# A fused attention and two-layer gated kernel: another computed order for the first half, and two first gates in banks of their own

## The chip, the cores and the metric

One NeuronCore of a Trainium2 chip runs the whole program. Its engines are TensorE (PE), VectorE (DVE), ScalarE (ACT), GpSimd (POOL) and SyncE (SP, which issues nearly all DMAs). Each takes its instructions in the order in which the program lists them and waits on semaphores. The metric is the device time of one execution in microseconds.

## The reference

```python
scores = scale * q @ k.T                     # (4 batch, 8 heads, 576, 576), head_dim 64
mask   = last 32 positions (heads 0-3) or last 32 of every 4th position (heads 4-7)
attn   = exp(scores - max); attn /= sum + 1e-9
x      = (attn @ v), heads side by side      # (2304 tokens, 512)
a = x @ w1;  b = x @ w2;  h = (a * b) @ w3   # 512 -> 1024 -> 1024
x = h @ w_out                                # 1024 -> 512
g = x @ w_gate                               # 512 -> 1536
out = (silu(g) * (x @ w_val)) @ w_out2       # 1536 -> 512
```

All is float32, and the kernel keeps more precision than one pass in float32r gives: each operand is split into a high and a low part, and each product is three matmuls (high x high, high x low, low x high), in the function `mm3`.

## The kernel before

Two heads make a pair; 4 batch rows of 4 pairs are the 16 units of attention. Only a band is computed: 9 blocks of 64 queries against 96 keys. A unit is: scores on PE (36 small matmuls into 2 banks), masks and maxima on DVE, exps on ACT, sums, inverse and normalisation on DVE or POOL, three groups of transposes on PE, copies of these on ACT (`pt`), values on PE (36 to 40 matmuls into 2 banks), and the evacuation into `x` in two parts (ACT the high, DVE the low; a copy to `beyond` for columns that belong to the next chunk). In the first batch row the last four of the nine softmax columns go by way of POOL and one wide exp (`WIDE`), and all normalisation is on DVE (`NORMV`); after it, normalisation is on POOL.

The tokens are taken in five chunks (4 of 512 columns and one of 256). For each chunk and each of 8 blocks k of 128 hidden units a gate is made: 12 matmuls of w1 and 12 of w2, 512 columns each (`gate`: ACT copies a to `ta`, DVE multiplies, ACT and DVE split the result to `p`), and `contraction` adds 12 matmuls with W = w3 @ w_out. W itself is made first on PE in two halves (`w_steps`, parts 0 and 1: 96 matmuls each, from 8 steps j times 4 banks), into the banks `acc` (bk_81 to bk_84), and copied out by ACT and DVE to W. The gates' banks are `ba` and `bb` (bk_85, bk_86); attention uses these and `batt` (bk_87, bk_88) until the first gate takes two away (`retire`).

Weights come as blocks of 1 MB (two weights each) in a packed form. `conversion` turns a block: a shift and a combining on DVE and a rescaling on ACT restore float32, then ACT makes the high and DVE the low part. The first two blocks go in halves of 512 columns. Buffers are `raw` (2) and `early` (2). Later blocks belong to the second layer: `quarter_block` restores them, forms sums (DVE), splits them into two `stages` (ACT and POOL) and stores them to DRAM, in `QUARTERS` portions by chunk.

The order of all this, up to the end of the third chunk, is not that of the source. `node` records each piece with an engine, a duration, what it comes after and a due time (`key`). `run_nodes` plays these through a list of events: each engine takes the ready piece with the least due time, and the pieces are then issued in the order in which they were started:

```python
                        for i in sorted(ready[e], key=lambda i: (wanted[i], i)):
...
                            started.append(i)
                            free[e] = t + x["us"]
```

The rest (`stage1` for the last two chunks, and the second layer, whose products go by a Strassen-like scheme of 7) is written out in the source's order. The second layer fills PE from about 420 us to the end and is not touched.

Of the kernel before, what the change touches and what calls it, by code (L numbers as in the profile page):

```python
# [50 lines left out]
W_BLOCKS = [("wo1", 0, 10), ("w3a", 0, 4), ("w1", 0, 0), ("w1", 1, 1), ("wo1", 2, 11), ("w3a", 2, 5), ("w1", 2, 2),  # L51
            ("wo1", 4, 6), ("w3a", 4, 8), ("w1", 3, 3), ("wo1", 6, 7), ("w3a", 6, 9),
# [36 lines left out]
QUARTERS = [2, 5, 5, 4, 2]  # L89
DMA_RATE = 0.31  # L90
FIRST, EACH, START = 4, 5, 36.0
W_AT = [24, 27]
# [4 lines left out]
def moe_chain_kernel(tc, q_in, k_in, v_in, w_in, mask_in, out):  # L97
# [8 lines left out]
    with static as st, other as ot, psum as pp, dram as dp:  # L106
# [142 lines left out]
        with att2_pool as a2:  # L249
# [239 lines left out]
            def node(engine, us, f, *args, after=(), key=INF, mb=0.0, take=None, give=None, retire=False):  # L489

                nodes.append(dict(
                    engine=engine, us=us, f=f, args=args, after=[a for a in after if a is not None], key=key, mb=mb,
                    take=take, give=give, retire=retire, got=None,
                ))
                return len(nodes) - 1
# [8 lines left out]

            def run_nodes(stock):
# [8 lines left out]
                ready = {}  # L514
                free = {}
# [7 lines left out]

                for i, x in enumerate(nodes):
                    ready.setdefault(x["engine"], [])
                    free[x["engine"]] = 0.0
                    if not left[i]:
                        push(0.0, "ready", i)
                done, started = 0, []
                while events:  # L530
                    t = events[0][0]
                    while events and events[0][0] <= t + 1e-9:
# [3 lines left out]
                        elif kind == "end":  # L536
                            done += 1
                            for g in nodes[i]["give"] or ():
                                src, items = g
# [8 lines left out]
                    for e in ready:  # L548
                        if free[e] > t + 1e-9:
                            continue  # L550
                        for i in sorted(ready[e], key=lambda i: (wanted[i], i)):
                            x = nodes[i]
                            if x["retire"] and any(b not in stock["bank"] for b in (2, 3)):
                                continue
                            if x["take"] and len(stock[x["take"][0]]) < x["take"][1]:
                                continue
                            if x["retire"]:
                                for b in (2, 3):
                                    stock["bank"].remove(b)
# [4 lines left out]
                            free[e] = t + x["us"]  # L564
                            push(free[e], "free", i)
                            if x["mb"]:
                                dma_free = max(t + 1.5, dma_free) + x["mb"] / DMA_RATE
                                push(dma_free + 1.0, "end", i)
                            else:
                                push(free[e] + 0.12, "end", i)  # L570
                            break
                assert done == len(nodes), [(nodes[i]["f"].__name__, nodes[i]["args"]) for i in range(len(nodes)) if i not in started][:9]
# [44 lines left out]
            raw_use = [None] * 4  # L617
# [3 lines left out]
            def conversion(n, key=INF, after=()):  # L621
# [4 lines left out]
                for b in range(2) if n < 2 else (None,):  # L626
                    bs = slice(0, 2) if b is None else slice(b, b + 1)
                    cols = 1024 if b is None else 512
                    ld = node("SP", 0.47, load_weights, n, b, after=[raw_use[r], *after], mb=cols / 1024, key=key)
# [9 lines left out]
                raw_use[r] = ends[-1]  # L639
# [35 lines left out]
            pt_use = [None]  # L675
            x_at, x_use = {c: [] for c in range(NC)}, {c: [] for c in range(NC)}
# [8 lines left out]
            def attention(i, t, dt, after=(), mask=None):  # L685

                b, hp = divmod(i, NPAIR)
                s_mm = node("PE", 1.05, scores, i, after=[loads["q", i], *s_use.get(sc_of(i), []), *after], key=t, take=("bank", 2))
# [653 lines left out]
```

## Time and profile before

| | |
|---|---|
| median of 3 runs | 835.08 us (833.55 to 836.95) |
| profiled execution | 835.79 us |
| span from the first to the last instruction in it | 834.0 us |
| mean granted clock of PE | 0.989 |
| PE busy | 807.8 us (97%) |
| DVE, ACT, POOL busy | 545.0, 423.6, 101.5 us |
| HBM read, written | 160.81 MB, 42.47 MB |

The span is cut into 40 slices of 20.85 us on the page. A line of waits says which instruction (engine, output, line) waited for which. In a timeline each row is a run of like instructions on one engine, and the bracket is the idle time ahead of it and what ended it. A product of 512 columns is listed with 0.39 us, since matmuls overlap; what counts is the distance from one start to the next.

### The profile page before, as it was taken

How to read it: one execution, taken by the hardware profiler on the slowest of the kernel's cores; microseconds unless marked ns; L12 is line 12 of the kernel's file. 1: busy time of each engine (PE TensorE's matmuls, PEld its weight loads, DVE VectorE, ACT ScalarE, POOL GpSimd, SP SyncE). 2: the span in 40 equal slices, each digit the busy share in tenths (PEclk: the TensorE clock that was granted, in tenths of full speed). 3: DMA queues.
4: the chain of work that ended last, by engine and by line, in shares of the span. 5: the costliest groups of instructions: out<-in, count | busy, mean ns of one | idle time of the engine just before them, and what ended most of it. 6: DMA issues, size and time to landing. Idle time of an engine off the chain costs nothing.

```text
span 834.0 us, 13900 instructions
## 1 busy us (share of the span) xinstructions
PE 807.8 (97%) x5242; PEld 732.4 (88%) x5242; DVE 545.0 (65%) x980; ACT 423.6 (51%) x975; POOL 101.5 (12%) x132
## 2 busy tenths in 40 slices
PE   6799999999999999999999999999999999999997
PEld 3677788878778788888999999999999999999997
DVE  5899967475668433475765737497746577564867
ACT  3877656666567544343554635363544354353432
POOL 1001102755554600000000000000000000000000
PEclk8799999999999999999999999999999999999999
DMA  8987454979789731277699777788978787977725
GB/s 237 313 324 257 142 185 140 301 274 319 233 311 329 246 100 73 80 247 234 233 310 386 250 253 264 244 323 277 307 251 253 246 259 244 316 270 246 252 83 176
DMA packets 80530, 204.18 MB, mean 245 GB/s; under 512 B 5840, under 2 KB 41808, under 8 KB 75856
## 3 DMA queue, kind: packets, MB, share of 16 engines
q1 hardware_dynamic: 78736, 200.68, 71.8%
q10 hardware_dynamic: 1728, 2.62, 0.9%
q8 instruction: 41, 0.67, 0.3%
q14 instruction: 25, 0.20, 0.1%
HBM read 160.81 MB, written 42.47 MB: 244 GB/s over the span
## 4 chain that ended last, share of the span: by engine, by line
PE 75%; DVE 11%; DMA 7%; ACT 3%; issue 2%; POOL 1%; SPq 0%; ACTq 0%; POOLq 0%; DVEq 0%
PE bk L195 24%; PE bk L197 23%; PE bk L196 23%; DMA raw<-w_in 6%; PE bk L382 2%; DVE raw L187 2%; PE bk L364 1%; DVE w L178 1%; PE bk L295 1%; DVE s L306 1%; DMA x2d<-o 1%; POOL stage L878 1%; DVE sm L318 1%; DVE early L187 1%; ACT s L323 1%
## 5 line engine op out<-in xcount | busy, mean ns | idle before, releaser
L195 PE MATMUL bk<-x,w 128*128 128x512 f32 (+2 forms) x400 | 147.1, 368 | 1.2 <-ACT ta L214 0.7
L197 PE MATMUL bk<-x,w 128*128 128x512 f32 (+2 forms) x400 | 144.8, 362 | 0.9 <-DVE w L178 0.9
L196 PE MATMUL bk<-x,w 128*128 128x512 f32 (+2 forms) x400 | 144.5, 361 | 0.0
L195 PEld LDWEIGHTS bk<-x,w 128*128 128x128 f32 x400 | 75.3, 188 | 12.3 <-ACT ta L214 0.9
L197 PEld LDWEIGHTS bk<-x,w 128*128 128x128 f32 x400 | 75.3, 188 | 11.7 <-DVE w L178 1.4
L1209 DVE TENSOR_TENSOR acc<-bk,acc 128x384 f32<-128x384 f32 x102 | 56.0, 555 | 44.3 <-PE bk L197 44.0
L196 PEld LDWEIGHTS bk<-x,w 128*128 128x128 f32 x400 | 75.4, 188 | 9.5
L197 PE MATMUL bk<-po,wo 128*128 128x384 f32 x240 | 80.5, 335 | 0.0
L196 PE MATMUL bk<-po,wo 128*128 128x384 f32 x240 | 80.2, 335 | 0.0
L195 PE MATMUL bk<-po,wo 128*128 128x384 f32 x240 | 79.4, 336 | 0.3 <-DVE acc L1209 0.3
L878 POOL TENSOR_TENSOR stage<-raw,stage 128x256 fp32r<-128x256 f32 x96 | 70.5, 767 | 37.4 <-ACT stage L876 37.4
L195 PE MATMUL bk<-w 128*128 128x384 f32 (+1 forms) x216 | 73.1, 341 | 0.0
L196 PE MATMUL bk<-w 128*128 128x384 f32 (+1 forms) x216 | 73.1, 338 | 0.0
L197 PE MATMUL bk<-w 128*128 128x384 f32 (+1 forms) x216 | 72.5, 339 | 0.0
L1134 ACT ACTIVATE u<-bk 128x384 f32<-128x384 f32 x80 | 38.6, 488 | 52.3 <-PE bk L197 52.3
L162 ACT ACTIVATE po<-u 128x768 fp32r<-128x768 f32 (+1 forms) x64 | 50.9, 803 | 26.3 <-PE bk L197 10.5
L163 DVE TENSOR_TENSOR po<-u,po 128x768 fp32r<-128x768 f32 (+1 forms) x64 | 57.5, 903 | 8.7 <-ACT po L162 8.6
L197 PE MATMUL bk<-p,W 128*128 128x512 f32 (+1 forms) x160 | 58.3, 369 | 0.0
L196 PE MATMUL bk<-p,W 128*128 128x512 f32 (+1 forms) x160 | 58.3, 369 | 0.0
L323 ACT ACTIVATE s<-s,sm 128x96 f32<-128x96 f32 x124 | 44.7, 363 | 26.3 <-DVE sm L318 26.3
L195 PE MATMUL bk<-p,W 128*128 128x512 f32 (+1 forms) x160 | 58.0, 379 | 0.0
L1148 ACT ACTIVATE g<-g 128x384 f32<-128x384 f32 x54 | 28.1, 521 | 40.2 <-DVE g L1143 40.1
(148 smaller groups left out, 1738.3 us busy)
## 6 DMA issues: line engine op xcount, KB each, us to landing
w<-wd SPq DMA_DIRECT2D x70, 512.0 KB, 4.6
wo<-wod SPq DMA_DIRECT2D x63, 512.0 KB, 4.6
raw<-w_in SPq DMA_DIRECT2D x28, 1024.0 KB, 7.4
mid<-wd SPq DMA_DIRECT2D x42, 512.0 KB, 4.6
wd<-stage SPq DMA_DIRECT2D x16, 896.0 KB, 4.9
early<-w_in SPq DMA_DIRECT2D x8, 1024.0 KB, 6.7
wod<-stage SPq DMA_DIRECT2D x8, 896.0 KB, 6.0
wd<-u SPq DMA_DIRECT2D x8, 896.0 KB, 5.1
```

The costliest lines, as they stand in the source:

```text
L162: nc.scalar.activation(hi, src, AF.Copy)
L163: return nc.vector.tensor_tensor(out=lo, in0=src, in1=hi.bitcast(F32), op=ALU.subtract)
L187: nc.vector.scalar_tensor_tensor(out=lo, in0=hi, scalar=3, in1=lo, op0=ALU.logical_shift_left, op1=ALU.bitwise_or)
L195: nc.tensor.matmul(ps, wh, xh, start=start, stop=False, skip_group_check=onto)
L196: nc.tensor.matmul(ps, wh, xl, start=False, stop=False, skip_group_check=onto)
L197: nc.tensor.matmul(ps, wl, xh, start=False, stop=stop, skip_group_check=onto)
L323: nc.scalar.activation(s[:, n], s[:, n], AF.Exp, bias=m[:, 0, n:n + 1], accum_out=m[:, 1, n:n + 1])
L382: nc.tensor.matmul(banks_of[got[w]][j * D:(j + 1) * D, lo - w * half:hi - w * half], v_of(i)[:KW, n, j * D:(j + 1) * D], pt[:KW, c, z * QB ...
L878: nc.gpsimd.tensor_tensor(out=dst[:, :, 1], in0=src, in1=dst[:, :, 0].bitcast(F32), op=ALU.subtract)
L1134: nc.scalar.activation(t, src, AF.Copy)
L1148: nc.scalar.activation(dst, src, AF.Silu)
L1209: nc.vector.tensor_tensor(out=a, in0=ps, in1=a, op=ALU.add)
```

## The change

The planner plays events by other rules, and some pieces are cut otherwise:

- Durations of scores, transposes and values are longer; PE's pieces take double time after a stretch with gaps; DMAs have two rates, and 8 of them at most are under way; each engine has its own latency to the next; DVE and POOL pieces marked `shared` are not started while the other engine holds such a piece.
- Due times get 40 sets of random shifts, each drawn from a seed in a list (`NUDGES`).
- The weights of w1 and w2 for k = 0, 1, 2 are loaded first, and three gates come before the first steps of W. The first two gates use bk_81 to bk_84 instead of bk_85 and bk_86, and each of their matmul groups is four pieces (3 matmuls) that need only one pair of heads each.
- `QUARTERS` goes from 2, 5, 5, 4, 2 to 3, 5, 5, 4, 1. The first gate of the fourth chunk and the last contraction of the third come into the planner, and the fourth chunk is drained through four buffers.

On DVE, in the softmax of the first pairs (s_107 is pair 0, s_116 pair 2; bk_87 and bk_88 hold pair 2's scores), the list before has:

```order
L351 RECIPROCAL sm_112<-sm_112 128x5
L306 SCALAR_TENSOR_TENSOR s_116<-bk_87,mask 128x384
L306 SCALAR_TENSOR_TENSOR s_116<-bk_87,mask 64x96
L306 SCALAR_TENSOR_TENSOR s_116<-bk_88,mask 128x384
L306 SCALAR_TENSOR_TENSOR s_116<-bk_88,mask 64x96
L356 TENSOR_TENSOR s_107<-s_107,sm_112 128x480
```

and now:

```order
L354 RECIPROCAL sm_112<-sm_112 128x5
L359 TENSOR_TENSOR s_107<-s_107,sm_112 128x480
L309 SCALAR_TENSOR_TENSOR s_116<-bk_87,mask 128x384
L309 SCALAR_TENSOR_TENSOR s_116<-bk_87,mask 64x96
L309 SCALAR_TENSOR_TENSOR s_116<-bk_88,mask 128x384
L309 SCALAR_TENSOR_TENSOR s_116<-bk_88,mask 64x96
```

Pair 0's last normalisation has moved ahead of pair 2's four mask steps.

Further on DVE, up to the last normalisation of the fourth pair (s_117; raw_77 and raw_78 are halves of loaded weights), before:

```order
L350 TENSOR_SCALAR sm_115<-sm_115 128x4
L351 RECIPROCAL sm_115<-sm_115 128x4
L185 TENSOR_SCALAR raw_77<-raw_77 128x512
L178 TENSOR_TENSOR W_74<-raw_77,W_74 128x512
L178 TENSOR_TENSOR w<-raw_78,w 128x512
L185 TENSOR_SCALAR raw_78<-raw_78 128x512
L350 TENSOR_SCALAR sm_115<-sm_115 128x5
L351 RECIPROCAL sm_115<-sm_115 128x5
L356 TENSOR_TENSOR s_117<-s_117,sm_115 128x384
L187 SCALAR_TENSOR_TENSOR raw_77<-raw_77 128x512
L187 SCALAR_TENSOR_TENSOR raw_78<-raw_78 128x512
L356 TENSOR_TENSOR s_117<-s_117,sm_115 128x480
```

and now:

```order
L353 TENSOR_SCALAR sm_115<-sm_115 128x4
L354 RECIPROCAL sm_115<-sm_115 128x4
L181 TENSOR_TENSOR w<-raw_77,w 128x512
L348 TENSOR_REDUCE sm_115<-s_117 128x5
L359 TENSOR_TENSOR s_117<-s_117,sm_115 128x384
L353 TENSOR_SCALAR sm_115<-sm_115 128x5
L354 RECIPROCAL sm_115<-sm_115 128x5
L188 TENSOR_SCALAR raw_77<-raw_77 128x512
L359 TENSOR_TENSOR s_117<-s_117,sm_115 128x480
```

Four of the six weight steps that stood between these softmax steps have gone behind them; a sum (TENSOR_REDUCE) now stands among them.

On PE, from the last transposes of pair 2 (s_116) through its values (v_104) to the first of the fourth pair (s_117), before:

```order
L364 MATMUL bk_88<-ident,s_116 96x128 x3
L382 MATMUL bk_85<-pt,v_104 64x64 x8
L382 MATMUL bk_86<-pt,v_104 64x32 x2
L382 MATMUL bk_85<-pt,v_104 64x32 x2
L382 MATMUL bk_86<-pt,v_104 64x64 x8
L195 MATMUL bk_81<-W_74,w 128x512
L196 MATMUL bk_81<-W_74,w 128x512
L197 MATMUL bk_81<-W_74,w 128x512
L195 MATMUL bk_82<-W_74,w 128x512
L196 MATMUL bk_82<-W_74,w 128x512
L197 MATMUL bk_82<-W_74,w 128x512
L364 MATMUL bk_87<-ident,s_117 96x128 x3
```

and now:

```order
L367 MATMUL bk_86<-ident,s_116 96x128 x3
L198 MATMUL bk_81<-x_76,w 128x512
L199 MATMUL bk_81<-x_76,w 128x512
L200 MATMUL bk_81<-x_76,w 128x512
L385 MATMUL bk_86<-pt,v_104 64x64 x8
L385 MATMUL bk_87<-pt,v_104 64x32 x2
L385 MATMUL bk_86<-pt,v_104 64x32 x2
L385 MATMUL bk_87<-pt,v_104 64x64 x8
L367 MATMUL bk_88<-ident,s_117 96x128 x3
L198 MATMUL bk_81<-x_76,w 128x512
L199 MATMUL bk_81<-x_76,w 128x512
L200 MATMUL bk_81<-x_76,w 128x512
```

Two groups of W's product (W_74 times w) are replaced by the first two pieces of the first gate (x_76 times w), one of which stands ahead of the values. The fourth pair's values come three groups of products after the list's start now, and four before.

The core of the diff:

```diff
-W_BLOCKS = [("wo1", 0, 10), ("w3a", 0, 4), ("w1", 0, 0), ("w1", 1, 1), ("wo1", 2, 11), ("w3a", 2, 5), ("w1", 2, 2),
-            ("wo1", 4, 6), ("w3a", 4, 8), ("w1", 3, 3), ("wo1", 6, 7), ("w3a", 6, 9),
+W_BLOCKS = [("w1", 0, 0), ("w1", 1, 1), ("w1", 2, 2), ("wo1", 0, 10), ("w3a", 0, 4), ("w1", 3, 3), ("wo1", 2, 11), ("w3a", 2, 5),
+            ("wo1", 4, 6), ("w3a", 4, 8), ("wo1", 6, 7), ("w3a", 6, 9),
...
-QUARTERS = [2, 5, 5, 4, 2]
-DMA_RATE = 0.31
+QUARTERS = [3, 5, 5, 4, 1]
+DMA_RATE = 0.285, 0.33
+LATENCY = {"PE": 0.16, "ACT": 0.1, "DVE": 0.09, "POOL": 0.05, "SP": 0.0}
...
-W_AT = [24, 27]
+EARLY = 18, 22
...
+            def nudge(seed):
+
+                r = np.random.default_rng(seed)
+                share, us = 10 ** r.uniform(-3, -0.7), 10 ** r.uniform(-0.3, 1.2)
+                kinds = list(range(len(nodes)))
...
+                m = r.random(max(kinds) + 1) < share
+                d = np.where(m, r.standard_normal(max(kinds) + 1) * us, 0.0)
+                return [float(d[k]) for k in kinds]
...
+                for seed in NUDGES:
+                    for i, d in enumerate(nudge(seed)):
+                        wanted[i] += d
...
+                            other = {"DVE": "POOL", "POOL": "DVE"}.get(e)
+                            if x["shared"] and held[other] > t + 1e-9:
+                                free[e] = held[other]
+                                push(free[e], "free", i)
+                                break
...
+                            if x["mb"]:
+                                free[e] = t
+                                for _ in range(x["dmas"]):
+                                    at = max(free[e], lanes.popleft())
+                                    free[e] = at + x["us"] / x["dmas"]
+                                    at = max(at + 1.5, dma_free)
+                                    dma_free = at + x["mb"] / x["dmas"] / DMA_RATE[at > 48]
+                                    lanes.append(dma_free + 1.0)
+                                push(lanes[-1], "end", i)
+                            else:
+                                free[e] = pe_end(t, x["us"]) if e == "PE" else t + x["us"]
+                                push(free[e] + LATENCY[e], "end", i)
...
+            def gate_banks(c, k):
+                return acc[2 * k:2 * k + 2] if c == 0 and k < 2 else (ba, bb)
+
+            def gate_mm(c, name, k, kts):
                 n = CHUNKS[c][1]
-                project((ba if name == "w1" else bb)[:, :n], (name, k), x_of(c)[:, :, :, :n])
...
+                x, w, ps = x_of(c)[:, :, :, :n], slot_of[name, k], gate_banks(c, k)[name == "w2"][:, :n]
+                for kt in kts:
+                    cs = slice(kt * P, (kt + 1) * P)
+                    mm3(ps, (w[:, 0, cs], w[:, 1, cs]), (x[:, 0, kt], x[:, 1, kt]), kt == 0, kt == KT - 1)
...
+                early = c == 0 and k < 2
+                ends = []
+                for w, name in enumerate(("w1", "w2")):
+                    i = None
+                    for kts in [(kt,) for kt in range(KT)] if early else [tuple(range(KT))]:
+                        before = [ready_at[name, k], i, *ends]
+                        before += pair_at[kts[0]] if early else [(ba_use, bb_use)[w][0], *x_at[c]]
...
             gates(0, 0)
             gates(0, 1)
-            for j in (2, 4):
+            gates(0, 2)
+            w_steps(0, (0,), next_at())
+            w_steps(0, (1,), next_at())
+            gates(0, 3)
+            for j in range(2, 6):
                 w_steps(0, (j,), next_at())
-                w_steps(0, (j + 1,), next_at())
-                gates(0, 2 + (j - 2) // 2)
...
             beyond_parts(4, at[0])
+            gate(3, 0, at[0], T)
+            contraction(2, K1 - 1, at[0] + 2 * T)
             run_nodes({"bank": [0, 1, 2, 3], "o": [0, 1]})
```

## Rows read from the trace of the kernel before

**Rows 1.** The page: span, and busy us (share) by engine.

```profile
span 834.0 us, 13900 instructions
...
PE 807.8 (97%) x5242; PEld 732.4 (88%) x5242; DVE 545.0 (65%) x980; ACT 423.6 (51%) x975; POOL 101.5 (12%) x132
```

**Rows 2.** Stretches: length, busy us of PE, PEld, DVE, ACT, POOL; clock, DMA share, GB/s.

```profile
31.00:38.00 7.00, 6.68 (x53) 5.66 (x54) 6.93 (x19) 6.24 (x11) 0.00 (x0) 0.53 0.89 235
...
54.00:78.00 24.00, 24.00 (x169) 19.70 (x169) 23.82 (x33) 19.19 (x35) 1.87 (x2) 1.00 0.78 277
```

**Rows 3.** PE waits from 46 us on: total us, times, longest.

```profile
PE bk L364 <- POOL s L356: 3.8, 2, 1.9
PE bk L195 <- DVE W L609: 1.6, 1, 1.6
PE bk L295 <- DVE beyond L418: 1.3, 1, 1.3
PE bk L195 <- ACT ta L214: 0.7, 1, 0.7
```

**Rows 4.** Timeline of PE in the head: start, us, instruction, idle before.

```profile
19.26 2.19 PE L382 MATMUL bk<-pt,v 96*64 96x64 f32 x36 [0.57 <-ACT pt L368]
...
35.10 0.63 PE L195 MATMUL bk<-W,w 128*128 128x512 f32 x1
35.52 0.63 PE L196 MATMUL bk<-W,w 128*128 128x512 f32 x1
...
40.19 1.39 PE L382 MATMUL bk<-pt,v 96*64 96x64 f32 x40 [0.69 <-ACT pt L368]
...
42.07 0.40 PE L197 MATMUL bk<-W,w 128*128 128x512 f32 x1
42.30 0.40 PE L195 MATMUL bk<-W,w 128*128 128x512 f32 x1
...
45.93 0.50 PE L197 MATMUL bk<-x,w 128*128 128x512 f32 x1 [0.94 <-DVE w L178]
```

**Rows 5.** Timeline of DVE in the head.

```profile
16.67 0.66 DVE L356 TENSOR_TENSOR s<-s,sm 128x480 f32<-128x480 f32 x1
...
23.30 1.45 DVE L306 SCALAR_TENSOR_TENSOR s<-bk,mask 128x384 f32<-128x384 f32 x4 [0.44 <-PE bk L295]
...
29.78 1.28 DVE L187 SCALAR_TENSOR_TENSOR raw<-raw 128x512 uint32<-128x512 uint32 x2
...
31.83 0.40 DVE L185 TENSOR_SCALAR raw<-raw 128x512 uint32<-128x512 uint32 x1
32.14 0.69 DVE L178 TENSOR_TENSOR W<-raw,W 128x512 fp32r<-128x512 f32 x1
...
35.62 0.65 DVE L356 TENSOR_TENSOR s<-s,sm 128x480 f32<-128x480 f32 x1
...
43.44 0.20 DVE L418 COPY beyond<-bk 128x32 f32<-128x32 f32 x1
```

**Rows 6.** Timeline of ACT in the head.

```profile
16.27 0.59 ACT L341 ACTIVATE s<-s 128x480 f32<-128x480 f32 x1
```

**Rows 7.** Timeline of DVE at 85 us.

```profile
85.06 2.48 DVE L609 TENSOR_TENSOR W<-bk,W 128x512 fp32r<-128x512 f32 x4
```

**Rows 8.** The chain that ended last, 150 to 180 us: start, us, what.

```profile
158.75 9.26 DMA raw<-w_in
```

**Rows 9.** ACT waits between 100 and 420 us.

```profile
ACT raw L183 <- DMA raw<-w_in: 23.1, 10, 4.6
```

**Rows 10.** Timeline of PE and of POOL, one pair of the second chunk.

```profile
189.22 1.04 PE L295 MATMUL bk<-k,q 64*64 64x96 f32 x36
...
194.96 0.99 POOL L356 TENSOR_TENSOR s<-s,sm 128x480 f32<-128x480 f32 x1 [1.98 <-DVE sm L351]
```

**Rows 11.** SP issues (start, us), and DMA issues (count, size, median us to landing).

```profile
12.35 4.54 SPq L597 DMA_DIRECT2D raw<-w_in  x4
...
raw<-w_in SPq DMA_DIRECT2D x4, 512.0 KB, 11.1
```

More of the change, by code (lines that the diff above doesn't have):

```diff
@@ L492, in node @@
                     engine=engine, us=us, f=f, args=args, after=[a for a in after if a is not None], key=key, mb=mb,
-                    take=take, give=give, retire=retire, got=None,
+                    take=take, give=give, retire=retire, got=None, dmas=1 + (f == load_qk), shared=engine == "POOL" or engine == "DVE" and f in (conv, inverse, normed, p_part, quarter_sum, bits, x1_part),
                 ))
@@ L522, in push, with may_start, pe_end @@
                     heapq.heappush(events, (t, seq, kind, i))
+                def may_start(x):
+                    if x["retire"] and not {2, 3} <= set(stock["bank"]):
+                        return False
+                    return not x["take"] or len(stock[x["take"][0]]) >= x["take"][1]
+                def pe_end(t, us):
+                    while us > 1e-9:
+                        w = int(t // STRETCH)
+                        pace = 0.5 if w and STRETCH - worked.get(w - 1, 0.0) > 1.6 else 1.0
+                        part = min((w + 1) * STRETCH - t, us / pace)
+                        worked[w] = worked.get(w, 0.0) + part
+                        us -= part * pace
+                        t = t + part if us <= 1e-9 else (w + 1) * STRETCH + 1e-12
+                    return t
                 for i, x in enumerate(nodes):
-                    ready.setdefault(x["engine"], [])
-                    free[x["engine"]] = 0.0
                     if not left[i]:
                         push(0.0, "ready", i)
-                done, started = 0, []
+                started = []
                 while events:
@@ L536, in run_nodes @@
                         elif kind == "end":
-                            done += 1
-                            for g in nodes[i]["give"] or ():
-                                src, items = g
+                            for src, items in nodes[i]["give"] or ():
                                 got = nodes[src]["got"]
@@ L563, in run_nodes @@
                             started.append(i)
-                            free[e] = t + x["us"]
-                            push(free[e], "free", i)
[L566 to L572, printed above, removed]
+                            if x["mb"]:
[10 more added lines that the diff above has]
+                                push(free[e] + LATENCY[e], "end", i)
+                            if x["shared"]:
+                                held[e] = free[e]
+                            push(free[e], "free", i)
+                assert len(started) == len(nodes)
                 with tc.manual_schedule(engines=set(ENGINES)):
@@ L614, in parts @@
                 return h, node("DVE", on_dve(n), dve_rest, lo, src, hi, after=[h], key=key, give=give)
-            raw_use = [None] * 4
+            raw_use = [[] for _ in range(4)]
             ready_at = {}
@@ L687, in attention @@
                 b, hp = divmod(i, NPAIR)
-                s_mm = node("PE", 1.05, scores, i, after=[loads["q", i], *s_use.get(sc_of(i), []), *after], key=t, take=("bank", 2))
+                s_mm = node("PE", 1.16, scores, i, after=[loads["q", i], *s_use.get(sc_of(i), []), *after], key=t, take=("bank", 2))
                 q_use[i] = s_mm
@@ L706, in attention @@
                 for g in range(3):
-                    tr = node("PE", 0.27, transposes, i, g, after=[x[0] if g == 0 else x[1], x[0], v_use.get(i - 1)], key=t + dt + 0.5 * g, take=("bank", 1))
+                    tr = node("PE", 0.35, transposes, i, g, after=[x[0] if g == 0 else x[1], x[0], v_use.get(i - 1)], key=t + dt + 0.5 * g, take=("bank", 1))
                     ts.append(tr)
@@ L710, in attention @@
                 s_use[sc_of(i)] = ts
-                v_mm = node("PE", 1.25, values, i, after=[*cp, loads["v", i]], key=t + dt + 3, take=("bank", 2))
+                v_mm = node("PE", 1.47, values, i, after=[*cp, loads["v", i]], key=t + dt + 3, take=("bank", 2))
                 v_use[i] = pt_use[0] = v_mm
@@ L827, in quarter_block @@
                         first_ends = ends
[L828 removed]
+                raw_use[r] = [node("SP", 0.01, stage_done, n, after=ends + first_ends)]
             def beyond_parts(c, key):
@@ L905, in moe_chain_kernel @@
                 conversion(n, after=[q_use[0]])
-            for j in range(2):
-                w_steps(0, (j,), W_AT[j])
             T = 2.95
```

106 lines of the change are left out of this document (60 added, 46 removed).

## The prediction

> **What bounds the kernel now.** I read the page first, then a table of stretches, PE's waits, and the timelines of the head. TensorE (PE) is busy 807.8 of 834.0 us [rows 1]. So the time is PE's work plus what PE loses, and this change leaves PE's work as it is: the number of scores, transposes, values and 128x512 products is the same, only their order and banks differ. The question is how many of the lost microseconds go.
>
> They are of three sorts. First the head, in which the first batch row's four pairs of heads go through attention. PE waits there for the softmax, and much of its time runs at the low level: 0.53 of the granted clock between 31 and 38 us [rows 2], that is mostly 1.2 of 2.4 GHz, after stretches with waits in them. Products there start 0.42 us apart, at full clock 0.23 [rows 4]. The head ends when the fourth pair's values (PE, 40.19) have been evacuated by VectorE (DVE), at 43.64 [rows 4, 5]. Second, from 46 us on, waits of 3.8, 1.6, 1.3 and 0.7 us [rows 3] and some smaller ones, which I leave aside. Third the end of the span, which the change doesn't reach.
>
> What sets the head's length is DVE. It is busy 6.93 of 7 us between 31 and 38, and 23.82 of 24 between 54 and 78 [rows 2]. It does two things by turns: softmax steps, for which PE waits, and the turning of loaded weights into two float32r parts, for which PE doesn't wait yet. Its queue is in order, so each weight step ahead of a softmax step delays PE.
>
> **The change part by part.**
>
> Pair 0's last normalisation moves ahead of the masks of pair 2 on DVE. It starts at 16.67 now, behind four mask steps of 1.45 us in sum [rows 5], so its transposes can go some 1.45 us sooner; ScalarE's (ACT) copies follow, and the exp of 0.59 us that stands between them now [rows 6] goes ahead of them all. By 1.45 + 0.59 I take 2.1 us for pair 0's values (19.26 now [rows 4]), and the fourth pair's scores, which stand right behind them, go with them. Its masks, at 23.30 now [rows 5], would start at about 21.2, 2.1 us sooner.
>
> From the end of these masks to the fourth pair's last normalisation, DVE's queue holds less weight work. Now there stand four shifts, four combinings and two subtractions of 512 columns; then two shifts, one combining and one subtraction. By 0.31 us for a shift, 0.60 for a combining and 0.60 for a subtraction (steps in rows 5, each less about 0.09, by which neighbours overlap) that is 2 x 0.31 + 3 x 0.60 + 0.60 = 3.0 us less. With the 2.1 before, that normalisation falls from 35.62 to about 30.5 if DVE never waits. The exps of ACT ahead of it should cost a part, so 31. From there to the values, 4.6 us pass now (35.62 to 40.19), two groups of six products at the low clock among them. The changed queue has two groups of three there, of which the first waits for pair 1's and the second for pair 2's x, and three copies of the transposes on ACT with a weight step between them. I take 5.0, and the values at 36.0: a gain of 4.2, by its bounds 1 (every us of weight work saved on DVE is lost again to ACT) and 5.1 (all of it arrives).
>
> PE has then done 9 products where it now has done 12, so three more remain, 3 x 0.23 = +0.7. The 0.9 us that PE waits at 45.93 for a weight [rows 4] goes, since weights of w1 and w2 are now loaded first; in its place the last pieces of the first gates wait for pair 3's x. That comes 2.0 us after the values' end now (41.58 to 43.64), and nine products, 2.1 us at full clock, stand before it: +0.3. Where the gates run at the low clock at first, they lose 0.19 each (0.42 - 0.23); now about eight do so (31 to 38 us), and I give the change +0.3 for more of them. Head: -4.2 + 0.7 - 0.9 + 0.3 + 0.3 = -3.8.
>
> A gate gives 24 products for one block of weights (1 MB), the product of two weights that now comes first 24 for two. With three gates first, DVE has fewer blocks to turn before PE can go on. That matters at 85 us, where DVE copies out four banks in a row (2.48 us) and PE waits 1.6 for the first [rows 3, 7]. From the end of the head to the first of these copies DVE now has 41.4 us to its name (43.64 to 85.06). The changed queue holds there 12 shifts and 12 combinings of 1024 columns, 11 subtractions, 7 steps of 512 and one set of masks. With the 512-column steps doubled, less the same overlap, that is 12 x 0.60 + 12 x 1.14 + 11 x 1.14 + 7 x 0.60 + 1.48 = 39.1 us. The head ending about 4 us sooner, the first copy would start at about 79, and PE goes on now when the first copy is done (85.06 and a quarter of 2.48), so it came 1.6 before, at 84.1; 3.8 us ahead of that is 80.3. The last copy, with three more weight pieces between the four, ends 5.7 us later, and PE comes to that bank after 21 products, 4.8 us: in time by half a microsecond. Of the wait of 1.6 I take 1.5 as gone. Bounds: 1.6 gone, or 0.5 added, if DVE waits for a gate on the way.
>
> The middle, 100 to 330 us. Here PE waits 3.8 us, in two waits of 1.9, for GpSimd's (POOL) normalisation and 1.3 for a bank [rows 3]. Behind the first I see a load of 1 MB that took 9.26 us (158.75) [rows 8]: ACT and DVE take its first steps in their order, wait, and the softmax of the next pair stands behind. ACT waits ten times for such loads, 23.1 us in all [rows 9], and few of these reach PE. The changed order begins with three of these blocks in the first chunk instead of two, and lets one fewer stand at the end, where nothing waits for it. It puts 24 products rather than 36 between scores and transposes in four places, but the first three transposes ask then for the half with four columns only. From scores to the first half normalised took 6.7 us (189.22 to 195.95) with five exps [rows 10], about 6.2 with four; 24 products and the scores cover 6.5. So this is as tight as before, and I take 4.0 us of waits instead of 5.1: -1.1. Bounds: all 5.1 gone, or four places at 1.9 each, +2.5.
>
> Nothing for the rest: the first gate of the fourth chunk now comes out of the same planner, and that chunk's last drain has four buffers instead of two, where PE waits 0.7 in all for a gate [rows 3] and not for a store.
>
> Sum: 834.0 - 3.8 - 1.5 - 1.1 = 827.6, and 1.8 us lie around the span (835.79 in that execution): 829.4. The median of the runs shown is 835.08, 0.7 lower, so 828.7.
>
> **A rule against it.** Between 31 and 38 us the clock stood at 0.53 with waits and short groups of products by turns [rows 2]. The Trainium skill (TensorE: Matmul & The Clock Gate, HAM oscillation) says that bursts with waits between them can find the slow clock each time anew. That speaks against three pieces of three products among the transposes; by it the first rival below is the likelier one, by the rows the forecast is, since eight slow products were enough in the kernel before.
>
> **The rivals.**
>
> 1. The low clock lasts. If all nine pieces, nine products of the second gate and eight more run 0.19 us slower, that is 4.9 us where eight products now lose 1.5: +3.4, so 832.1. For it: pieces and waits alternate until pair 3's x is there. Against it: the nine pieces run while PE would wait anyway. 0.12.
>
> 2. The first piece holds up PE. It stands ahead of pair 2's values and wants a weight whose load is issued at about 12.35 and lands 11.1 us later by the median [rows 11], at 23.5 (both for the four halves of the kernel before); the changed ACT queue comes to it at about 22.3, ahead of pair 1's copies. At a landing at 25.3 it costs 3.0 us of the head: 831.7. Against it: half a megabyte less is queued ahead of it than before. 0.08.
>
> 3. All goes: the head at its best (5.1 - 0.7 + 0.9 = 5.3), the wait of 1.6, and the 5.1 of the middle. 834.0 - 12.0 + 1.8 - 0.7 = 823.1; with one of the three middle waits left, 825. 0.18.
>
> 4. The other side: loads in the middle. If the shorter covers let ACT's waits for loads through to PE, each at its mean of 2.3 us (23.1 / 10), seven of them make 16.1 us instead of my 4.0: 840.8. It decides from five on (11.5 us, 836). For it: 9 us loads, a third block in the first chunk. Against it: of ten such waits about three arrived. 0.07.
>
> **How the numbers follow.** The forecast, 825 to 831.5 by its own bounds, has 0.55, the rivals 0.12, 0.08, 0.18 and 0.07. What a measurement can tell from no change is 0.5%, 4.2 us: below 830.9 is faster, above 839.3 slower. Faster: 0.55 less a tail of 0.01, and 0.18: 0.72. Same: rivals 1 and 2, that tail and the smaller cases of rival 4: 0.23. Slower: 0.05. The range runs from rival 3 to past rivals 1 and 2: 822.5 to 834.5; it leaves out rival 4 and a little of rival 3.
>
> **What would show it.** The fourth pair's values on PE at about 36 instead of 40.2, and its last evacuation at about 38.5 to 39.5; eight to fifteen products of the gates at 0.42 us; no wait for the copies of W at 79 to 86, and the two groups of scores after the gates; PE's waits between 100 and 330 us near 4 us in all. The prediction is wrong if the values come later than 39, if PE waits over 1.5 us for weights between 40 and 90, or if the middle's waits exceed 8 us.

## The result, and the profile after

| | before | changed |
|---|---|---|
| median, beside each other | 834.41 us (833.55 to 836.95, 4 runs) | 825.55 us (824.70 to 827.83, 4 runs) |
| ratio, 95% interval | | 0.9897 [0.9875, 0.9918] |
| profiled execution, span | 835.79 us, 834.0 us | 827.83 us, 826.0 us |

The change saves 8.9 us by the medians. The forecast was 828.7 us, a gain of 6.4. The profiled execution is the slowest of its four, and it saves 8.0. The page of the changed kernel, against [rows 1]:

```profile
PE 809.1 (98%) x5242; PEld 732.9 (89%) x5242; DVE 546.9 (66%) x972; ACT 424.0 (51%) x975; POOL 103.5 (13%) x140
```

PE's work is the same, so the gain is in what PE loses. PE's busy time by stretches (start and end, length, busy, clock, DMA share, GB/s), before:

```profile
0.00:46.00 46.00, 32.58 (x373) 0.81 0.86 277
46.00:100.00 54.00, 52.02 (x290) 1.00 0.72 256
100.00:330.00 230.00, 224.64 (x1725) 1.00 0.68 228
...
430.00:460.00 30.00, 29.50 (x183) 1.00 0.97 360
```

and changed:

```profile
0.00:46.00 46.00, 37.42 (x396) 0.81 0.87 282
46.00:100.00 54.00, 53.65 (x297) 1.00 0.69 251
100.00:330.00 230.00, 228.49 (x1742) 1.00 0.74 245
...
430.00:460.00 30.00, 27.66 (x153) 0.94 0.86 293
```

With the stretch that is left out (330 to 430 us), PE is idle for 8.6, 0.35, 1.5, 0.3 and 2.3 us in the changed kernel. Before it was idle for 13.4, 2.0, 5.4, 0.7 and 0.5 us, with the clock at 1.00 from 46 us on. The differences: head -4.8, the stretch with the copies of W -1.6, middle -3.9, then -0.4, and +1.8 behind 430 us, where the clock of 0.94 also costs 1.8 (30 x 0.06). The warm-up products ahead of the first scores, which count as busy, took 4.77 instead of 5.85 us: -1.1. Sum -8.2, of a span that is 8.0 shorter.

PE's waits from 46 us on in the changed kernel, against [rows 3]:

```profile
PE bk L198 <- ACT g L1214: 2.3, 1, 2.3
PE bk L367 <- ACT pt L371: 1.1, 1, 1.1
```

The waits for POOL (3.8), for the copies of W (1.6) and for a gate (0.7) are gone. Waits of the same two sorts, for silu and for a copy of transposes, were 0.5 and 0.3 us before. PE in the head, against [rows 4]:

```profile
6.15 1.04 PE L298 MATMUL bk<-k,q 64*64 64x96 f32 x36
...
16.80 2.19 PE L385 MATMUL bk<-pt,v 96*64 96x64 f32 x36 [0.58 <-ACT pt L371]
...
34.44 1.41 PE L385 MATMUL bk<-pt,v 96*64 96x64 f32 x40 [0.16 <-ACT pt L371]
...
38.85 0.50 PE L199 MATMUL bk<-x,w 128*128 128x512 f32 x1 [0.35 <-DVE x L654]
```

Pair 0's values start at 16.80 (19.26), the fourth pair's at 34.44 (40.19), and the only wait behind them is 0.35 us for pair 3's x. DVE, against [rows 5, 7]:

```profile
20.84 1.45 DVE L309 SCALAR_TENSOR_TENSOR s<-bk,mask 128x384 f32<-128x384 f32 x4 [0.55 <-PE bk L298]
...
30.11 0.65 DVE L359 TENSOR_TENSOR s<-s,sm 128x480 f32<-128x480 f32 x1
...
38.71 0.19 DVE L421 COPY beyond<-bk 128x32 f32<-128x32 f32 x1
...
79.53 1.29 DVE L654 TENSOR_TENSOR W<-bk,W 128x512 fp32r<-128x512 f32 x2
...
84.81 0.68 DVE L654 TENSOR_TENSOR W<-bk,W 128x512 fp32r<-128x512 f32 x1
```

The fourth pair's masks come at 20.84 (23.30), its last normalisation at 30.11 (35.62), the last evacuation at 38.71 (43.44), the first copy of W at 79.53. Stretches, against [rows 2]:

```profile
31.00:38.00 7.00, 6.81 (x82) 5.16 (x79) 6.66 (x16) 6.87 (x13) 0.00 (x0) 1.00 0.75 186
438.00:442.00 4.00, 4.00 (x16) 4.00 (x15) 1.54 (x3) 0.49 (x1) 0.00 (x0) 0.57 1.03 403
```

Between 31 and 38 us the clock is 1.00 instead of 0.53: the low level of 1.2 GHz ended at 28.6 us in this execution, and no gate product ran at it. A new low stretch stands at 438 us.

The place at 437 us, ACT first, then PE:

```profile
436.21 0.38 ACT L240 ACTIVATE o<-bk 128x256 f32<-128x256 f32 x1 [4.48 <-DMA x2d<-o]
436.49 0.48 ACT L1214 ACTIVATE g<-bk 128x384 f32<-128x384 f32 x1
```

```profile
437.03 0.45 PE L198 MATMUL bk<-x,w 128*128 128x384 f32 x1 [2.34 <-ACT g L1214]
```

The fifth chunk's drain has two buffers. Its third copy waits 4.48 us until the first store has landed, and the silu for which PE waits is queued behind it. Before, the first and the third copy were 7.5 us apart (439.23 and 446.74), with five other pieces between them, and the copy waited 1.79; here they are 5.9 apart (430.31 and 436.21), with one.

### The profile page after: what moved, and what is told of

Read it like the earlier page. It is cut to its first block, busy times and chain, and to the rows that moved or that the text cites. A ratio compares the mean times of both kernels' runs of the same rounds, so it can differ in the third digit from the quotient of the medians.

```text
span 826.0 us, 13914 instructions
## 1 busy us (share of the span) xinstructions
PE 809.1 (98%) x5242; PEld 732.9 (89%) x5242; DVE 546.9 (66%) x972; ACT 424.0 (51%) x975; POOL 103.5 (13%) x140
## 4 chain that ended last, share of the span: by engine, by line
PE 78%; DMA 8%; DVE 8%; ACT 3%; issue 2%; POOL 1%; SPq 0%; ACTq 0%; DVEq 0%; POOLq 0%
PE bk L198 25%; PE bk L200 24%; PE bk L199 24%; DMA raw<-w_in 5%; PE bk L385 2%; PE bk L298 1%; PE bk L367 1%; DVE raw L190 1%; DMA wod<-stage 1%; DVE w L181 1%; DVE s L309 1%; DMA wd<-stage 1%; DMA x2d<-o 1%; DVE raw L188 1%; DMA raw<-x2d 1%
## 5 line engine op out<-in xcount | busy, mean ns | idle before, releaser
L198 PEld LDWEIGHTS bk<-x,w 128*128 128x128 f32 x400 | 75.6, 189 | 13.4 <-ACT g L1214 2.7
L945 POOL TENSOR_TENSOR stage<-raw,stage 128x256 fp32r<-128x256 f32 (+1 forms) x104 | 74.2, 745 | 61.6 <-ACT stage L943 57.0
L186 ACT ACTIVATE raw<-raw 128x1024 f32<-128x1024 f32 (+1 forms) x32 | 34.8, 1097 | 27.6 <-DMA raw<-w_in 27.6
```

The costliest lines, as they stand in the source:

```text
L186: nc.scalar.activation(hi.bitcast(F32), hi.bitcast(F32), AF.Prelu, scale=REBIAS, alpha=SIGN_UP)
L198: nc.tensor.matmul(ps, wh, xh, start=start, stop=False, skip_group_check=onto)
L945: nc.gpsimd.tensor_tensor(out=dst[:, :, 1], in0=src, in1=dst[:, :, 0].bitcast(F32), op=ALU.subtract)
```

## The experiments

All are timed against runs of the kernel before on the same chip; four chips were used. How well medians repeat is seen from the changed kernel, which gave 825.55 and, run again later, 825.45.

**The kernel before, once more.** No edit.

> The kernel before, once more. The fourth pair's values came 5.75 us sooner in the changed kernel (40.19 to 34.44), but the first scores already 1.1 us sooner (7.24 to 6.15), since the 14 warming products took 4.77 us instead of 5.85, though nothing in the change touches them. Theory 1 (the start varies from one execution to the next): the warming products of this run can take another time than 5.85 us, and where they end sooner the values of the fourth pair come sooner by no more than that. Theory 2 (the start is a part of the change, by the mask's load that goes behind the first k and q): 5.85 us again, and first scores at 7.2.

836.24 us. The warm-up products took 5.17 us, so theory 1 holds. The first scores start at 6.56 (7.24), the fourth pair's values at 39.12 (40.19); the waits in the middle stand where they stood. So about 0.7 us of the head differ by the start of an execution alone, and what follows is counted from the first scores: 32.95 and 32.56 us to the fourth pair's values before, 28.29 after.

**The changed kernel without the rank changes.**

```diff
-NUDGES = [2000001, 2000025, 2000032, ...]
+NUDGES = []
```

> The changed kernel without the 40 sets of rank changes: new blocks, gates in pieces, new rules, but the plain due times. Theory 1 (the head's gain comes from the order on VectorE, which the rank changes make, and so does a good part of the middle's): the fourth pair's values come at 36 to 39 instead of 34.4, and there are 3 to 6 us of waits on TensorE between 46 and 420 us instead of 2.1: 829 to 833 us. Theory 2 (it comes from the gates in pieces and the weights' order, and the rank changes are small): values within 1 us of 34.4, and 825 to 828 us.

833.64 us (832.67 to 839.29, 10 runs), ratio 0.9989 [0.9968, 1.001]: no gain. From scores to values 31.98 us. Its waits from 46 us on:

```profile
PE bk L367 <- POOL s L359: 3.5, 3, 2.4
PE bk L367 <- ACT pt L371: 2.4, 2, 2.0
PE bk L367 <- DVE ta L788: 1.3, 1, 1.3
```

The wait for the copies of W is gone here too. In the middle (100 to 330 us) PE is idle for 7.2 us, more than before (5.4). The low clock lasts to 36.2 us, and the first three gate products run at it. So with the new pieces the head and the middle owe their gain to the recorded rank changes.

**The new blocks, pieces and banks under the old planner.**

```diff
 def run_nodes(stock):
-    (DVE and POOL by turns, two load rates, clock at gaps, rank changes)
+    (as in the kernel before, with its durations and DMA_RATE = 0.31)
```

> The new blocks, the gates in pieces with banks of their own, the new portions by chunk and the last chunks' changes, but the order is computed by the rules of the kernel before (one load rate, no shared access, no clock, one latency, its durations) and without rank changes. Theory 1 (the order on VectorE decides, and the rules make it): little of the gain is left, 830 to 836 us, with fourth values later than 37 and 4 to 8 us of waits from 46 to 420 us. Theory 2 (what is loaded first and how the gates are cut decides): 825 to 829 us.

837.71 us (833.81 to 842.87, 10 runs), ratio 1.0028 [1.0008, 1.0048]. Its waits:

```profile
PE bk L367 <- POOL s L359: 3.4, 2, 1.9
PE bk L367 <- ACT pt L371: 2.6, 1, 2.6
```

The low clock lasts to 41.1 us here, and seven gate products run at it. The new blocks, pieces and banks save nothing by themselves.

**The old blocks, pieces and banks under the new planner,** without rank changes.

```diff
 def run_nodes(stock):
-    (as in the kernel before)
+    (DVE and POOL by turns, two load rates, clock at gaps; no rank changes)
```

> The kernel before, its blocks, gates and portions, with only the new rules and durations of the planner, without rank changes. Theory 1: the rules alone give a part, 829 to 834 us, and the wait at the copies of W stays near 1.6 us, since W is still made first. Theory 2: no change, 833 to 836 us.

832.08 us (830.92 to 832.91, 4 runs), ratio 0.9956 [0.9941, 0.997]. Its waits:

```profile
PE bk L366 <- ACT pt L370: 2.3, 1, 2.3
...
PE bk L199 <- DVE W L180: 0.7, 2, 0.6
```

The rules alone give about 3.4 us, none in the head (the values start at 41.66). POOL's waits go, and PE's idle time in the middle falls from 5.4 to 2.1 us. The wait for the copies of W goes too, against theory 1, though W is still made first; the 0.7 us listed are waits for weights being turned (0.4 before). The new rules with the new pieces and no rank changes gave 833.64, so the two don't add.

**Pair 0's last normalisation back behind pair 2's masks,** all else in the changed kernel's order.

```diff
 DVE: ...
-pair 0 normalised (5 columns); pair 2 masks x4
+pair 2 masks x4; pair 0 normalised (5 columns)
```

> The changed kernel with one instruction moved: on VectorE pair 0's last normalisation goes back behind pair 2's masks; everything else keeps the changed kernel's order. Theory (the head is set by in-order softmax steps, so what stands ahead of one delays all behind): pair 0's values start 1.5 to 2 us later than 16.80 (less the start's own variation), the fourth pair's scores and masks with them, its values near 36 instead of 34.44, and the kernel takes 1.0 to 2.0 us more, 826.5 to 827.5. Rival (VectorE has slack in the head, the later steps catch up): the fourth pair's values stay within 0.5 us of 34.44 and the time is that of the changed kernel, 825.5.

828.86 us (826.10 to 831.11, 4 runs), ratio 0.993 [0.9905, 0.9955]. PE in its head:

```profile
6.27 1.04 PE L298 MATMUL bk<-k,q 64*64 64x96 f32 x36
...
18.30 2.19 PE L385 MATMUL bk<-pt,v 96*64 96x64 f32 x36 [0.58 <-ACT pt L371]
...
36.60 1.41 PE L385 MATMUL bk<-pt,v 96*64 96x64 f32 x40
```

One instruction moved puts pair 0's values from 10.65 to 12.03 us behind the first scores; before they were 12.02 and, in the second profile, 12.95 behind. The term is 1.4 us. The fourth pair's values come 30.33 us behind the first scores, against 28.29, but a later profile of the changed kernel has 30.33 too. Whether the whole kernel pays more than 1.4, as the median says (3.3), is open: its interval and the changed kernel's overlap.

**Five weight steps ahead of the fourth pair's last normalisation.**

```diff
 DVE: ...
+2 shifts, 3 combinings of 512 columns (blocks 0 and 1 of w_in)
 pair 3 normalised (5 columns)
-(the same five, behind)
```

> The changed kernel with five weight steps of the first two blocks of w_in (two shifts, three combinings of 512 columns, 2.4 us together) moved on VectorE from behind to ahead of the fourth pair's last normalisation. Theory (each us of weight work ahead of that normalisation is a us of the head): the normalisation starts near 32.5 instead of 30.11, the fourth pair's values near 36.8 instead of 34.44, and the kernel takes about 2 us more, 827 to 828. Rival (VectorE or TensorE waits for something else there, such as exps on ScalarE): values within 0.5 us, the time unchanged at 825.5. Second rival: the wait lets the clock fall, more than 3 us.

827.84 us (826.45 to 829.01, 4 runs), ratio 0.9919 [0.99, 0.9937], 2.3 us above the changed kernel, with intervals that overlap. DVE and then PE:

```profile
33.19 0.65 DVE L359 TENSOR_TENSOR s<-s,sm 128x480 f32<-128x480 f32 x1
```

```profile
34.30 0.53 PE L367 MATMUL bk<-ident,s 128*96 128x128 f32 x3 [2.65 <-DVE beyond L421]
...
37.83 1.91 PE L385 MATMUL bk<-pt,v 96*64 96x64 f32 x40
```

The normalisation falls from 30.11 to 33.19, PE waits 2.65 us, for a copy out of a bank that stands behind it on DVE, and the clock falls once more (the values take 1.91 instead of 1.41): from first scores to values 31.58 us instead of 28.29, 3.3 more. The medians differ by 2.3; other waits differ too (1.2 us for the copies of W, and 0.6 instead of 2.3 at 437 us), so how much of the head arrives isn't settled. The theory's mechanism is there, its size in the head was a little low.

**The half of five blocks first** in softmax and normalisation of four pairs of the middle; PE still transposes the half of three (the first group) first.

```diff
 maxima, exps, inverse, normalised, for pairs 6, 8, 9, 11:
-half of 4 columns; half of 5 columns
+half of 5 columns; half of 4 columns
```

> The changed kernel with the half of five blocks put ahead of the half of three in maxima, exps, inverse and normalisation of pairs 6, 8, 9 and 11 (in the middle, where 24 products stand between a pair's scores and its first transposes). Theory A (the smaller half first is what makes 24 products enough: normalised 0.4 us before the transposes need it): four waits of some 2 us for GpSimd at about 152, 189, 222 and one more place, 6 to 9 us more, 831.5 to 834.5. Rival B (the halves' order costs only where GpSimd's queue is full): at most 3 us more, 826 to 828.5.

832.07 us (829.95 to 834.41, 10 runs), ratio 0.9966 [0.995, 0.9981], 6.5 us above the changed kernel. In the changed kernel one of these places reads so (PE, POOL, PE):

```profile
146.26 1.04 PE L298 MATMUL bk<-k,q 64*64 64x96 f32 x36
...
152.83 0.49 PE L367 MATMUL bk<-ident,s 128*96 128x128 f32 x3
```

```profile
151.61 0.83 POOL L359 TENSOR_TENSOR s<-s,sm 128x384 f32<-128x384 f32 x1 [1.58 <-DVE sm L354]
```

The half is normalised at 152.44, 0.4 us before PE wants it. With the halves exchanged there are four waits:

```profile
PE bk L367 <- POOL s L359: 5.1, 4, 1.4
```

Theory A holds as to the total, by waits of 1.05 to 1.40 instead of 2 us. Between 100 and 330 us PE is idle for 5.6 us instead of 1.5, so 4.1 of the 6.5 are there; the rest isn't assigned. It is a test of the order of the halves together with PE's order, not of either alone.

**The last drain through four half-sized buffers.**

```diff
-drain(..., bufs if c == 3 else None)
+drain(..., bufs if c == 3 else [ost[m % 2][:, m // 2 * n:(m // 2 + 1) * n] for m in range(KT)])
```

> The changed kernel with its last chunk of the first layer's output drained through four half-sized buffers instead of two whole ones; the planner's order of some second-layer evacuations shifts with it. Theory (the new wait of 2.34 us at 437 us comes from the third drain copy, which waits 4.48 us on ScalarE for a store to free its buffer, with silu behind it in the queue): the wait goes and the time falls by about 2 us, to 823 to 824. Rival (another wait takes its place, since evacuation of that chunk is late anyway): unchanged, 825 to 826.

825.87 us (824.84 to 828.26, 6 runs), ratio 0.99 [0.9883, 0.9917]: unchanged, as the rival said. ACT, then PE:

```profile
430.37 3.71 ACTq L243 DMA_DIRECT2D x2d<-o  x4
434.12 0.49 ACT L1214 ACTIVATE g<-bk 128x384 f32<-128x384 f32 x1 [3.43 <-DMA x2d<-o]
```

```profile
434.67 0.44 PE L198 MATMUL bk<-x,w 128*128 128x384 f32 x1 [1.41 <-ACT g L1214]
```

No copy waits any more, but all four stores now stand in a row on ACT's queue, and silu still stands behind them. The row of 3.71 us runs from the start of the first issue to the end of the last; each issue in it takes 0.33 to 0.44. Its longest part is a pause: the last copy was done at 431.6, and the fourth store was issued at 433.75. The chain of work says what it waited for:

```profile
427.29 6.38 DMA mid<-wd
```

That is a load issued by SP, which landed at 433.67. The store waits on a semaphore on which this load had counted, and then uses it itself. So the next expectation is wrong where it says that the issue itself took 3.71 us; the queue was held by a wait.

**The same, with the four stores issued by GpSimd.** PE's and SP's order are the changed kernel's.

```diff
-nc.scalar.dma_start(out=dst(m), in_=o)
+store.dma_start(out=dst(m), in_=o)      # last chunk: store = nc.gpsimd
```

> The changed kernel with two edits to the drain of the last chunk: four half-sized buffers as before, and its four stores issued by GpSimd, which has nothing else to do there, instead of ScalarE. TensorE's and SyncE's order are those of the changed kernel. Theory (ScalarE's queue is held by the stores: with two buffers a copy waits for one to land, with four their issue itself took 3.71 us, and silu stands behind either): TensorE's wait near 437 us (2.34, and 1.41 with four buffers) goes, the low clock at 438 to 442 us with it, and the kernel takes 823.5 to 824.8. Rival (something else, such as VectorE's products or a late load, holds the same place): a wait of over 1 us stays near 437 us and the time is 825.5 to 826.5.

823.62 us (822.83 to 824.99, 4 runs), ratio 0.987 [0.9854, 0.9887]. All waits of PE from 46 us on:

```profile
PE bk L298 <- DVE beyond L421: 0.6, 1, 0.6
PE bk L198 <- DVE acc L1275: 0.3, 1, 0.3
PE bk L199 <- DVE p L166: 0.2, 1, 0.2
```

The wait at 437 us and the low clock behind it are gone. The four stores take 2.33 us on GpSimd's queue, 0.54 to 0.71 each, without a pause. This is the fastest version; against its neighbour it is 1.8 us by the medians, with intervals that overlap.

**The changed kernel once more.** No edit.

> The changed kernel once more, timed beside the others of this call. By theory its profile has the fourth pair's values within 0.5 us of 34.44 (less the start's variation), 1 to 2.5 us of wait near 437 us, and a median of 825 to 827; by the rival that the first look was lucky, 828 or more.

825.45 us (823.85 to 829.83, 4 runs), ratio 0.9884 [0.9864, 0.9904]. Its profile is not like the first. ACT, then PE:

```profile
24.12 0.69 ACT L186 ACTIVATE raw<-raw 128x512 f32<-128x512 f32 x1 [1.80 <-DMA raw<-w_in]
```

```profile
6.87 2.23 PE L298 MATMUL bk<-k,q 64*64 64x96 f32 x72
...
25.22 0.88 PE L367 MATMUL bk<-ident,s 128*96 128x128 f32 x3 [1.30 <-ACT pt L371]
...
31.48 0.63 PE L199 MATMUL bk<-x,w 128*128 128x512 f32 x1
...
37.20 1.40 PE L385 MATMUL bk<-pt,v 96*64 96x64 f32 x40 [0.15 <-ACT pt L371]
```

ACT waits 1.80 us (0.56 in the first profile) for the first load of w_in, with pair 1's copies queued behind it. PE waits for those, the low clock lasts to 33.4 us, and the fourth pair's values come 30.33 us behind the first scores instead of 28.29.

**The first weights turned later,** on top of the version with the stores on GpSimd, to take that wait away.

```diff
 ACT: ...
-x0; w step 1; copies of pair 1 x2; w step 4; copy; 2nd half's step 1; exps of pair 3
+x0; copies of pair 1 x3; w step 1; exps of pair 3; w step 4; (2nd half's step 1 behind pair 2's copies)
 DVE: ...
-shift; pair 2 normalised; combining; sums; maxima x2; pair 2 normalised
+pair 2 normalised; sums; maxima x2; shift; pair 2 normalised; combining
```

> The kernel with the four stores on GpSimd, with the first block of w_in turned later: on ScalarE its first step goes behind pair 1's three copies and its fourth behind pair 3's exps, the second half's first step behind pair 2's copies; on VectorE its shift and its combining go behind pair 3's maxima and pair 2's second normalisation. TensorE's and SyncE's order stay. Theory (in the runs with a long head ScalarE waits 1.8 us for this block's load, with pair 1's copies queued behind it; and weight steps ahead of softmax steps lengthen the head anyway): from the first scores to the fourth pair's values 27.3 to 28.3 us in any execution, against 28.29 and 30.33 in the two looks at the changed kernel, and the time falls by 1 to 2.5 us against its neighbour in this call, to 821.0 to 822.6. Rival (the first products then wait for these weights and TensorE loses as much there): a wait of over 0.5 us ahead of the first products at about 29 us, the time unchanged within 0.7 us.

825.16 us (824.11 to 826.77, 5 runs), ratio 0.9883 [0.9866, 0.9901], against 824.52 of its neighbour: the theory fell. ACT waits for no load in the head, and yet scores to values take 30.22 us (7.42 to 37.64). DVE, then PE, then the clock in a stretch of the head:

```profile
22.10 1.46 DVE L309 SCALAR_TENSOR_TENSOR s<-bk,mask 128x384 f32<-128x384 f32 x4 [0.55 <-PE bk L298]
...
31.55 0.65 DVE L359 TENSOR_TENSOR s<-s,sm 128x480 f32<-128x480 f32 x1
```

```profile
28.79 2.38 PE L367 MATMUL bk<-ident,s 128*96 128x128 f32 x9 [0.77 <-DVE x L687]
...
32.37 2.36 PE L385 MATMUL bk<-pt,v 96*64 96x64 f32 x40
```

```profile
20.00:34.00 14.00, 11.83 (x129) 0.50 1.03 359
```

From the masks to the last normalisation DVE takes 9.45 us, as in the first profile of the changed kernel (20.84 to 30.11, 9.27): the moved steps still stand ahead of that normalisation, so the row is no shorter. And a new wait of 0.77 stands at 28.8, after which the low clock lasts to 34.6 us; in the changed kernel's first profile it ended at 28.6. The rival's wait ahead of the first products didn't come either.

**The version with the stores on GpSimd once more.** No edit.

> The kernel with the four stores on GpSimd once more, as the neighbour of the other run of this call. By theory its median is 823 to 824.5 and no wait stands near 437 us; by the rival that the first look was lucky, 825 to 826. From the first scores to the fourth pair's values it takes 28.2 to 28.4 us if the first load lands before ScalarE wants it, and 30.0 to 30.4 if not.

824.52 us (823.30 to 826.01, 5 runs), ratio 0.9873 [0.9852, 0.9895], with no wait at 437 us. Its scores to values take 29.51 us (6.08 to 35.59) after a wait of 1.0 for the load: between the two sizes that I had named. In the six profiles with this order of the head, the wait for the load and the head go together: 28.3 us with waits of 0.56 and 0.61, 29.5 with 0.99, and 30.0 to 30.3 with 1.51 to 1.83. That the load is the cause is not shown, since the version without this wait took 30.22 too.

## Why the prediction was right, and where not

**Head, forecast -3.8.** Right in mechanism and near in size. By the first profiles it was -4.8 and a start 1.1 shorter; from first scores to the fourth pair's values the two profiles of the kernel before give 32.95 and 32.56, the two of the changed one 28.29 and 30.33, so -2.2 to -4.7. Of the steps: pair 0's normalisation ahead of the masks was to save 2.1 and saved 1.4 (12.03 against 10.65 with one instruction moved): the exp of 0.59 that I added to the 1.45 did not come on top. The weight work taken from ahead of the last normalisation was to save 3.0: from the masks to that normalisation it was 12.3 us in both profiles before, and 9.27 and 10.15 after. Putting some back delayed that normalisation by 3.1 us and made the head 3.3 longer. The wait at 45.93 is gone.

**The low clock, +0.3 and rival 1.** "Eight to fifteen gate products" at the low level was too many: none in the first profile, the three of the first piece in the second (31.48, 0.63 us). Rival 1's price did not come in this order; where the low clock lasted longer, transposes and values paid. In the same pieces without the rank changes, three and seven gate products did run at it. The low level that the head starts with ended near 29 us in the three profiles with pair 1's transposes in one run and no wait ahead of pair 2's. In the five with a wait at either place (0.50 to 1.30 us) it ended between 31.8 and 34.6 us. In the run with pair 0's normalisation put back the clock rose at 22.0 us, fell again at 25.4 in a wait of 1.91 (24.7 to 26.6), and rose for good at 32.2. That agrees in kind with the rule of the Trainium skill (TensorE: Matmul & The Clock Gate, HAM oscillation). But the waits were the softmax's; the pieces of gates, run while PE would have waited, showed no harm in the changed order.

**Rival 2** happened in part, unforeseen in its place: the late load held up ACT's copies for pair 1 (1.80 us), not PE at the first piece.

**Copies of W, -1.5.** Right in size: no wait of PE is left there in the first profile, and 0.2 to 0.7 us are left in four of the five others with this order up to there (the forecast had it in time by half a microsecond). The first copy was forecast at 79 and stands at 79.53, the last ends 6.0 us later (forecast 5.7). That the three gates ahead of W are the reason is not shown: the old blocks under the new rules have no such wait either.

**Middle, -1.1.** Right in sign, too small: PE's idle time fell by 3.9, nearer to the bound of -5.1. The step that failed is "as tight as before". 24 products and the scores cover 6.57 us (146.26 to 152.83), the half is normalised after 6.18, and the slack of 0.4 held at three such places (152.83, 189.27, 222.56), in two profiles each. With the new pieces it takes the rank changes (without them POOL's waits are 3.5) and the half with four columns first (the other way round four waits, 5.1). With the old pieces the new rules alone did nearly as much for the middle (2.1 us idle). ACT's waits for loads stay, 21.1 us in 14 against [rows 9], and no wait of PE there is put down to a load:

```profile
ACT raw L186 <- DMA raw<-w_in: 21.1, 14, 4.6
```

Rival 4 needed five of them to do so.

**"Nothing for the rest"** is the step that was wrong. I considered the fourth chunk's drain, which got four buffers, and not the fifth's, which keeps two and whose copies now stand closer together on ACT. It cost 2.34 us of waiting and 1.7 of low clock (4.0 x 0.43) in the first profile, and 0.6 to 2.5 of waiting in others with that drain. The clock fell behind it in the two profiles of the changed kernel alone; the wait of 2.5, in the run with the halves exchanged, left it at 1.00. With the stores off ACT's queue the wait is gone, and the medians are lower by 1 to 2 us, which the intervals don't settle.

So the forecast missed -2.8 in the middle and +3.5 at 437 us, which nearly cancel in the profiled execution. That the total came so near is luck in this part. Which of the 40 rank changes do the work was not tried.

## What to carry to other kernels

With engines that work in order, a step that nobody waits for costs what stands behind it; that holds for softmax behind weight steps, and for silu behind a copy or a store that waits. When an order computed from a model is changed, look again at the first piece written out behind it: there the copies, the buffers and the stores meet in a new rhythm. And rules or cuts may give little or nothing without the rest (833.64, 837.71 and 832.08 us) where rules, cuts and rank changes together give 825.5: test them apart before one of them gets the credit.

## What was not expected of the hardware

- The 14 warm-up products, the first work of PE, took from 4.68 to 6.03 us in executions of kernels with the same rows there. They start 0.43 us apart at first and 0.22 later; 7 run at the wider distance in the shortest case, nearly all in the longest. That moves the head by up to 1.3 us and is no effect of a change.
- A store of 128 KB takes 0.33 to 0.44 us to be issued on ACT's queue and 0.54 to 0.71 on GpSimd's. What holds an engine's queue is the wait ahead of a store: 2.0 us ahead of the fourth in a row, ended by the landing of a load issued on another queue.
- One order can have heads 2 us apart: the first load landed 1.2 us later from the first scores on, PE had one more short wait (1.30 us), and the low clock ended at 33.4 instead of 28.6 us.
